# Issue order and spreading of the side work in the sequence stage of a gated Fourier and GEGLU kernel

## The chip, the cores and the metric

The kernel runs on one core of one Trainium2 chip. The metric is the device time of one execution in microseconds; the time before is the median of three runs. All arithmetic is float32, done on TensorE (PE) as three products of split numbers: each operand is a high part and a low part, and a product of two split operands is three matmuls (high by high, low by high, high by low). VectorE is DVE, ScalarE is ACT, GpSimd is POOL, SyncE is SP; SP does nothing here but issue DMAs.

## The reference

```python
x = A_x                                   # 1 x 2048 x 640
g = sigmoid((x * gate_w).sum(-1, keepdims=True))
a = einsum("bsd,ed->bse", x, dft_hid_re)
b = einsum("bsd,ed->bse", x, dft_hid_im)
A = einsum("ts,bse->bte", dft_seq_re, a) - einsum("ts,bse->bte", dft_seq_im, b)
B = (gelu(x @ w_gate) * (x @ w_up)) @ w_down        # F = 1728
return g * A + (1 - g) * B
```

## The kernel before

The kernel computes products in 2 by 2 blocks by a Strassen scheme with seven products, so each stage needs sums and differences of its operands ahead of its matmuls. It has four stages, one after the other on PE:

- **Gate and up** (line 1238): 13 blocks of F. The last one, `f = 12`, also prepares the next stage: its DVE and ACT side jobs wait in the list `fills`, and `fill` (line 1214) lets them out in step with PE, by their written costs (`state["all"]`, `state["pe_all"]`): a job is let out when the cost done so far is at most 1.25 x all x pe / pe_all. Within this stage the order on PE, ACT, DVE and POOL is the written one.
- **C stage** (line 1368): the sequence DFT applied to x, with the products kept in HBM (`uA`, and their sums `uT`). It has 64 steps: four groups of 16 (cosine or sine, and two halves of t). In a group the first eight steps (`b = 0`, "first half") have 30 matmuls each and use the x factors `xa`; the last eight (`b = 1`, "second half") have 24 and use `xb`. A step `i` needs its two tiles of DFT matrix c(i), 512 KB each.
- **K stage** (line 1505): the down projection, from h (`hA`, `hT`) and `w_down` (`wd`, and its sums `wsd`).
- **U stage** (line 1563): the hidden DFT, from `uA`, `uT`, `wu` and its sums `wsu`, and the mix of both branches.

**A C step.** In step `i` the program writes `load_c(i + 3)` (line 772: two loads on SP), then `split_c(i + 2)` (line 779: in a first-half step two high parts on ACT, line 80, and two low parts on DVE, line 83; in a second-half step also four differences on DVE into `csa` and `csb`, lines 785 to 789), then the 10 or 8 products of step `i`. In the first eight steps it also loads and splits the x factors: `fetch_xn` loads (line 739), `split_xa` makes three differences on DVE, a high part on ACT, and the low part by a negation on ACT and an accumulating DMA on POOL (`by_dma`, line 754); `whole=True` would make the low part on DVE.

**The transition in a group.** The last first-half step (`held`, line 1394) is written otherwise: PE does X, ACT copies X out of PSUM, then comes `prepare` (the split of c(i+2), whose high parts are on ACT), then the other products, then ACT copies Z and L out. The first second-half step needs PSUM banks that these copies free (`pQ`). ACT and DVE run in written order in this stage, so the copy of Z stands behind the high parts of c(i+2), and these stand behind what DVE has ahead of their differences. PE, POOL and SP have no written order here: the framework's scheduler places their instructions by its own estimate, with each instruction allowed ahead of an earlier one when its tile is free.

**Units.** The C stage also does side work for the later stages. A unit's loads are written in one step and its DVE work in the next step (`ready`, line 1373), behind `prepare`, with stores on POOL:

- T sums of h (`sum_h`, line 615): four loads of 256 KB, four DVE sums, four stores. Steps by `HT_AT`, four units for each of the last three groups.
- weight sums (`sum_wd`, line 608): loads `dr` (512 KB) and `da`, four DVE sums, four stores to `wsd`. Steps by `WD_AT`, two for each of these groups.
- logits (`load_z`, line 719): a load `xz` of 320 KB and one DVE reduction. Steps by `ZC_AT`.
- `sum_wu` (line 679): loads `ur` and `ua`, sums, stores to `wsu`; in steps `WU_AT` and the next.

Behind each second half DVE forms the group's results and, in the next step, `tsums` (line 1486), which POOL stores to `uA` and `uT`.

**Tiles.** Loads wait for free tiles: tag `s4` has 46 (c, x factors, `dr`, `xz`), tag `m` has 15 (`ht`, `ur`, the group's results), tag `w` has 6 (`da`, `ua`).

`in_order(SP)` (line 106) adds an edge from each SP instruction traced inside it to the next one, so that the scheduler must keep the written order; nothing is added on the chip.

Of the kernel before, what the change touches and what calls it, by code (L numbers as in the profile page):

```python
# [21 lines left out]
NP = NS // 2  # L22
NF = F // P
# [4 lines left out]
PAIRED = 3  # L28
ZB_AT = [5,7,9,14,15,16]
XB_AT = [0, 1, 2, 3, 4, 5, 6, 7]  # L30
WU_AT, WU_DOWN = [18, 34, 50], [10, 17]
HL_AT = [1, 12]


# [1 line left out]
def kernel(  # L36
# [636 lines left out]
    def store_left():  # L673
        for to, v in left_out:
            nc.sync.dma_start(to, v)
        left_out.clear()
# [62 lines left out]
    def fetch_xn(sp):  # L739

        r, s = xraw[sp] = tuple(slot(F32, [P, 4, 256], f"x{k}{sp}") for k in "nm")
        nc.sync.dma_start(r[:, 0:3], xn[sp, :, 0:3])
        nc.sync.dma_start(s[:, 0:2], xn[sp, :, 3:5])
# [259 lines left out]
    loads = ExitStack()  # L1003
# [208 lines left out]
    fills, state = deque(), {}  # L1212
# [24 lines left out]
    with in_order(PE, ACT, DVE, POOL):  # L1237
        for f in range(1, NF):
            kind = pair_of(f)
            if f == PAIRED:  # L1240
                loadu()
                fills.extend([*t4, *u123[:3], *late_work, *u123[3:], *u4])
            fills.extend(todo)
            todo.clear()
            if kind == 1:
                up, work = make_up(f, load_up(f))
                fills.extend(work)
            if f == PAIRED - 1:
                loadp()
                fills.extend(t123)  # L1250
            if f + 1 < NF:
                nxt, work = make_w(f + 1)
                if kind != 1 or f == PAIRED:
                    fills.extend(work)
            if kind == 1 and f > PAIRED:
                fills.extend(work)
            if f == NF - 1:
                for k in range(2):
                    fetch_xn(k)
                    load_c(k)  # L1260

                def made():
                    sums_made.pop(0)()

                for k in range(2):
                    fills.extend([(126, partial(split_xa, k)), (122, made), (245, partial(split_c, k))])
            state.update(pe=0, done=0, all=sum(c for c, _ in fills), pe_all=2450 if not kind else 2994 if kind == 1 else 1768)
            s5 = pair(F32, f"s5{f}")
            xs = {}
            work = [gate_up(f, W, Bs[tp], tp, s5[:, tp], s1t, xs, s4) for tp in range(2)]  # L1270
            more = together(f, W, Tp, s1t, xs) if kind == 1 else iter(())
            more_up = together_up(f, W, up, s4) if kind == 1 else iter(())
            store_left()
            if f == 2:
                k = len(fills) // 2
                rest = [fills.pop() for _ in range(len(fills) - k)]
                fills.extend([*sum_h0(0), *sum_h0(1), *reversed(rest)])
                state["all"] = sum(c for c, _ in fills)
            for _ in range(4):
                run(more)  # L1280
            for step in range(8 if not kind else 7):
                for tp, w in enumerate(work):
                    run(w)
                    if (step, tp) in ((0, 1), (1, 1)):
                        run(more)
                        if step == 0:
                            run(more)
                    if (2, 0) < (step, tp) < (6, 0):
                        run(more_up)
                if step < 2 and kind == 1 and f > PAIRED:  # L1290
                    for k in ((1,), (2, 3))[step]:
                        load_across(f, "xu", Tu, keptu, k)
                if step == 4 and pair_of(f + 1) == 1 and f + 1 > PAIRED:
                    for k in (1, 2, 3):
                        load_across(f + 1, "xq", Tp, keptp, k)
                if step == 5:
                    load_w(f + 2)
                if f == NF - 1 and step == 5:
                    fetch_xn(2)
                    load_c(2)  # L1300
            for v in (more, more_up):
                next(v, None)
            while fills:
                fills.popleft()[1]()
            W = nxt
# [49 lines left out]
    def put(to, i, src):  # L1355
        nc.gpsimd.dma_start(to[:, i], src)

    HT_AT, WD_AT, ZC_AT = {}, {}, [17, 22, 30, 33, 38, 46, 49, 53, 54, 62]
    for g in range(3):
        for q, r in enumerate((2, 3, 4, 13)):  # L1360
            HT_AT[16 * g + 16 + r] = q % 2, 2 * g + q // 2
        for q in range(2):
            WD_AT[16 * g + 18 + 2 * q] = 2 * g + q
    units = []
    X = Z = V = L = Q = R = Y = None
    sv, wus = {}, {}
    store_left()
    for i, (j, ri, b, sp) in enumerate(cseq):
        if i + 3 < NP:
            fetch_xn(i + 3)  # L1370
        if i + AHEAD + 1 < len(cseq):
            load_c(i + AHEAD + 1)
        ready, units = units, []
# [4 lines left out]
        if i in ZC_AT:  # L1378
            (_, first), (_, total) = load_z(1)
            first()  # L1380
            units.append(total)
        if i + 2 < NP:
            split_xa(i + 2, False)
        for _ in range(XB_AT.count(i)):
            split_xb(xleft.pop(0))

# [56 lines left out]
        else:  # L1443
# [21 lines left out]
            if lst:  # L1465
# [32 lines left out]
                        put(to, 3, t4)  # L1498

                after.append(tsums)  # L1500


    zwork, narrow = [], []
    gates(0)
# [266 lines left out]
```

## Time and profile before

| | us |
|---|---|
| median of three runs (lowest, highest) | 1059.74 (1057.55, 1061.1) |
| profiled execution, its own time | 1058.28 |
| span of that execution, first to last instruction | 1056.5 |
| PE busy in the span | 1024.0 |
| DVE, ACT, POOL busy | 823.8, 487.9, 185.0 |
| C stage on PE, first c matmul to first K matmul | 331.02 to 762.08 |
| mean granted TensorE clock | 0.989 |

A row of the waits view reads: who waited, for whom, total us, times, longest us. A row of the windows view reads: stretch in us from the span's start, its length, then busy us of PE, PEld, DVE, ACT and POOL with their number of instructions, the granted clock, the DMA share and GB/s. A row of the timeline reads: start, duration, engine, line, operation, out<-in, count, and in brackets the idle time before it with what ended it; an SP row is the issue of a DMA. A row of the groups reads: line, engine, operation, out<-in and shapes, count, then busy us and mean ns, then idle us before. A row of the issues view ends with the size of one transfer and the median us from issue to landing.

### The profile page before, as it was taken

To read this page: it belongs to the slowest core of one execution; us is meant where nothing else is said; L and a number is where in the kernel's file an instruction comes from. 1 tells how busy PE (TensorE), PEld (TensorE's weight loads), DVE (VectorE), ACT (ScalarE), POOL (GpSimd) and SP (SyncE) were. 2 spreads that over 40 slices of the span, in tenths; PEclk is the share of its full clock that TensorE was granted. 3 is DMA by queue.
4 is the path that set the end of the run, shared out by engine and by line. 5 is a ranking of instruction groups with operands and counts; after the bars stand their busy time and mean duration, and the time that the engine had idled before them with its cause. 6 is when DMAs were issued, how large, how long until landed. Compare 5 with 4: busy or idle time off the path is not lost.

```text
span 1056.5 us, 13360 instructions
## 1 busy us (share of the span) xinstructions
PE 1024.0 (97%) x4489; PEld 839.9 (79%) x4489; DVE 823.8 (78%) x1158; ACT 487.9 (46%) x625; POOL 185.0 (18%) x327
## 2 busy tenths in 40 slices
PE   9999999999999999996999799998999999999998
PEld 7888888888888778885888678876888878888887
DVE  8977755474759689767887798789989797996796
ACT  6644535444436654423343244324537636654340
POOL 0221111111301110223023301240120111011112
PEclk9999999999999999999999989998999999999999
DMA  8465455454669956898789877999899999987856
GB/s 308 146 213 193 126 179 166 152 167 147 195 208 331 252 163 231 263 385 308 258 283 384 340 265 256 382 413 361 294 327 372 412 391 341 391 316 218 269 151 100
DMA packets 101332, 281.47 MB, mean 266 GB/s; under 512 B 13520, under 2 KB 24656, under 8 KB 101264
## 3 DMA queue, kind: packets, MB, share of 16 engines
q1 hardware_dynamic: 73536, 194.15, 52.4%
q0 software_dynamic: 27440, 86.28, 25.7%
q8 instruction: 35, 0.57, 0.2%
q14 instruction: 33, 0.27, 0.1%
q10 hardware_dynamic: 288, 0.20, 0.1%
HBM read 205.06 MB, written 70.27 MB: 261 GB/s over the span
## 4 chain that ended last, share of the span: by engine, by line
PE 62%; issue 16%; DMA 16%; DVE 3%; POOL 2%; ACT 0%; SPq 0%; POOLq 0%; DVEq 0%
DMA ht<-hA 4%; PE pX L99 4%; PE pX L101 4%; PE pX L100 4%; DMA xz<-in_xz 4%; PE pZ L101 3%; PE pZ L100 3%; PE pZ L99 3%; DMA cra<-in_ct 2%; DMA crb<-in_ct 1%; DMA uA<-s 1%; PE kX L99 1%; PE kX L101 1%; PE kX L100 1%; PE kL L100 1%
## 5 line engine op out<-in xcount | busy, mean ns | idle before, releaser
L80 ACT ACTIVATE ch<-csa 128x1024 fp32r<-128x1024 f32 x32 | 34.0, 1062 | 123.8 <-DVE csa L786 102.0
L80 ACT ACTIVATE ch<-cra 128x1024 fp32r<-128x1024 f32 x32 | 33.9, 1059 | 78.8 <-DMA cra<-in_ct 32.9
L83 DVE TENSOR_TENSOR cl<-cra,ch 128x1024 fp32r<-128x1024 f32 x32 | 39.1, 1221 | 24.1 <-ACT ch L80 15.8
L415 POOL DMA_DIRECT2D hA<-s x48 | 26.1, 545 | 177.6 <-DVE s L582 158.0
L415 POOL DMA_DIRECT2D hT<-ht x48 | 26.0, 541 | 144.4 <-DVE ht L623 134.6
L99 PE MATMUL pL<-ch,xah 128*128 128x512 f32 x128 | 50.0, 391 | 0.5 <-DVE sa L1469 0.5
L100 PE MATMUL pL<-cl,xah 128*128 128x512 f32 x128 | 49.8, 389 | 0.0
L101 PE MATMUL pL<-ch,xal 128*128 128x512 f32 x128 | 49.0, 389 | 0.0
L571 DVE TENSOR_TENSOR s<-s,pX 128x512 f32<-128x512 f32 x24 | 16.4, 685 | 38.5 <-PE pX L101 38.5
L83 DVE TENSOR_TENSOR cl<-crb,ch 128x1024 fp32r<-128x1024 f32 x32 | 39.1, 1222 | 9.1 <-ACT ch L80 3.8
L80 ACT ACTIVATE ch<-crb 128x1024 fp32r<-128x1024 f32 x32 | 33.8, 1057 | 25.0 <-PE pL L100 10.3
L83 DVE TENSOR_TENSOR cl<-csa,ch 128x1024 fp32r<-128x1024 f32 x32 | 39.0, 1220 | 2.9 <-ACT ch L80 2.5
L99 PE MATMUL pQ<-ch,xbh 128*128 128x512 f32 x64 | 26.7, 417 | 13.9 <-ACT s L146 13.9
L83 DVE TENSOR_TENSOR cl<-csb,ch 128x1024 fp32r<-128x1024 f32 x32 | 39.2, 1224 | 0.7 <-PE pY L100 0.2
L557 ACT ACTIVATE s<-pZ 128x512 f32<-128x512 f32 x24 | 14.2, 597 | 52.2 <-PE pZ L101 35.3
L576 ACT ACTIVATE s<-s 128x512 f32<-128x512 f32 x24 | 15.1, 633 | 46.8 <-DVE s L575 46.8
L80 ACT ACTIVATE ch<-csb 128x1024 fp32r<-128x1024 f32 x32 | 33.9, 1060 | 6.2 <-DVE csb L789 5.2
L99 PE MATMUL pX<-ch,xbh 128*128 128x512 f32 x64 | 25.6, 406 | 9.7 <-ACT ch L80 6.3
L146 ACT ACTIVATE s<-pX 128x512 f32<-128x512 f32 x41 | 23.7, 593 | 24.5 <-PE pX L101 24.2
L83 DVE TENSOR_TENSOR kl<-kw,kh 128x1024 fp32r<-128x1024 f32 x24 | 29.3, 1223 | 5.4 <-ACT kh L80 5.4
L80 ACT ACTIVATE kh<-kw 128x1024 fp32r<-128x1024 f32 x24 | 25.5, 1063 | 16.2 <-DMA kw<-wsd 13.8
L99 PEld LDWEIGHTS pL<-ch,xah 128*128 128x128 f32 x128 | 24.0, 188 | 6.3 <-DVE sa L1469 1.3
(3658 smaller groups left out, 3475.1 us busy)
## 6 DMA issues: line engine op xcount, KB each, us to landing
cra<-in_ct SPq DMA_DIRECT2D x64, 512.0 KB, 5.9
crb<-in_ct SPq DMA_DIRECT2D x64, 512.0 KB, 7.0
hA<-s POOLq DMA_DIRECT2D x48, 256.0 KB, 3.0
ht<-hA SPq DMA_DIRECT2D x48, 256.0 KB, 8.3
hT<-ht POOLq DMA_DIRECT2D x48, 256.0 KB, 6.9
kr<-hA SPq DMA_DIRECT2D x24, 512.0 KB, 7.4
kr<-hT SPq DMA_DIRECT2D x24, 512.0 KB, 8.3
ux<-uA SPq DMA_DIRECT2D x24, 512.0 KB, 7.3
```

Source lines behind the costliest of these rows:

```text
L80: nc.scalar.activation(hi, raw, AF.Copy)
L83: nc.vector.tensor_tensor(lo, raw, hi.bitcast(F32), op=ALU.subtract)
L99: nc.tensor.matmul(ps, lh, rh, start=first, stop=False, skip_group_check=True)
L100: nc.tensor.matmul(ps, lh, rl, start=False, stop=False, skip_group_check=True)
L101: nc.tensor.matmul(ps, ll, rh, start=False, stop=last, skip_group_check=True)
L146: nc.scalar.activation(m, src, AF.Copy)
L415: nc.gpsimd.dma_start(to[:, i], src)
L557: nc.scalar.activation(s5, Z, AF.Copy)
L571: tt(s5, s5, X, op=ALU.add)
L576: nc.scalar.activation(s2, s2, AF.Gelu_apprx_tanh)
```

## The change

Five edits, all for the C stage:

1. SP keeps the written order from the first to the last step of the C stage.
2. T sums: the places in a group move from steps 2, 3, 4 and 13 to 2, 4, 8 and 13. Weight sums: from 2 and 4 to 3 and 5.
3. Logits: from steps 17, 22, 30, 33, 38, 46, 49, 53, 54, 62 to 16, 22, 26, 32, 38, 42, 48, 54, 58, 60 (in places of a group: 1, 6, 14 / 1, 6, 14 / 1, 5, 6, 14 become 0, 6, 10 / 0, 6, 10 / 0, 6, 10, 12). The third `sum_wu` moves from step 50 to 49.
4. The third x factor `xa[2]` is made in the last block of gate and up, with its low part on DVE; two entries (126 and 122) join the six of `fills`. Its loads go out at step 3 of that block and those of x factor 3 at step 5.
5. In the C stage the x factors are loaded four steps ahead and split three steps ahead, each one step earlier than before.

```diff
-WU_AT, WU_DOWN = [18, 34, 50], [10, 17]
+WU_AT, WU_DOWN = [18, 34, 49], [10, 17]
...
                 for k in range(2):
                     fills.extend([(126, partial(split_xa, k)), (122, made), (245, partial(split_c, k))])
+                fills.extend([(126, partial(split_xa, 2)), (122, made)])
...
+                if f == NF - 1 and step == 3:
+                    fetch_xn(2)
                 if f == NF - 1 and step == 5:
-                    fetch_xn(2)
                     load_c(2)
+                    fetch_xn(3)
...
-    HT_AT, WD_AT, ZC_AT = {}, {}, [17, 22, 30, 33, 38, 46, 49, 53, 54, 62]
+    HT_AT, WD_AT, ZC_AT = {}, {}, [16, 22, 26, 32, 38, 42, 48, 54, 58, 60]
     for g in range(3):
-        for q, r in enumerate((2, 3, 4, 13)):
+        for q, r in enumerate((2, 4, 8, 13)):
             HT_AT[16 * g + 16 + r] = q % 2, 2 * g + q // 2
         for q in range(2):
-            WD_AT[16 * g + 18 + 2 * q] = 2 * g + q
+            WD_AT[16 * g + 19 + 2 * q] = 2 * g + q
...
     store_left()
+    loads = ExitStack()
+    loads.enter_context(in_order(SP))
     for i, (j, ri, b, sp) in enumerate(cseq):
-        if i + 3 < NP:
-            fetch_xn(i + 3)
+        if i + 4 < NP:
+            fetch_xn(i + 4)
...
-        if i + 2 < NP:
-            split_xa(i + 2, False)
+        if i + 3 < NP:
+            split_xa(i + 3, False)
...
                 after.append(tsums)
-
+    loads.close()
```

## The prediction, made before the change was run

> **What bounds the kernel now.** I read the page first, then the waits of PE, then a table by half groups of the C stage, and last the queues around one stall.
>
> ```profile
> PE 1024.0 (97%) x4489; PEld 839.9 (79%) x4489; DVE 823.8 (78%) x1158; ACT 487.9 (46%) x625; POOL 185.0 (18%) x327
> ```
>
> PE is the bound, so only time in which PE idles or runs slowly can be gained. Its waits, longest in total first:
>
> ```profile
> PE pQ L99 <- ACT s L146: 13.9, 2, 7.4
> PE pX L99 <- ACT ch L80: 6.3, 2, 6.0
> PE pX L99 <- ACT s L146: 3.4, 3, 1.5
> PE pX L101 <- DMA xal<-xn: 2.3, 2, 1.6
> ```
>
> All are in the C stage, on tiles that first appear where a first half turns into a second half, or on an x factor's low part. The windows by half groups (first and second half of each group; the third row is a stretch without stalls):
>
> ```profile
> 331.02:389.84 58.82, 56.54 (x247) 45.93 (x246) 44.40 (x65) 35.77 (x38) 7.45 (x10) 1.00 0.81 228
> 389.84:434.71 44.87, 44.10 (x193) 35.88 (x192) 39.76 (x47) 22.97 (x27) 2.22 (x4) 1.00 0.67 226
> 402.07:434.71 32.64, 32.64 (x145) 27.03 (x144) 27.65 (x32) 15.78 (x18) 0.00 (x0) 1.00 0.62 207
> 434.71:490.63 55.92, 54.57 (x241) 44.86 (x240) 42.85 (x62) 15.59 (x17) 20.01 (x37) 1.00 1.00 351
> 490.63:544.31 53.68, 45.99 (x193) 37.35 (x193) 43.44 (x55) 22.95 (x27) 4.87 (x9) 0.94 0.78 261
> 544.31:600.95 56.64, 54.86 (x241) 44.78 (x240) 45.07 (x65) 15.78 (x17) 20.54 (x38) 1.00 1.00 371
> 600.95:653.60 52.65, 45.91 (x193) 37.30 (x194) 43.18 (x55) 22.50 (x27) 4.32 (x8) 0.90 0.72 251
> 653.60:709.25 55.65, 54.86 (x242) 44.78 (x240) 44.98 (x65) 17.42 (x22) 21.45 (x40) 1.00 1.02 384
> 709.25:762.08 52.83, 46.52 (x192) 37.74 (x193) 48.91 (x63) 24.66 (x29) 4.49 (x9) 0.94 0.92 339
> ```
>
> The third row gives 32.64 / 144 = 0.2267 us a matmul without a stall (six steps of 24). A first half of 240 matmuls then takes 54.40, a second half of 192 takes 43.52. So the halves lose, in order: 3.06 (six gate and up matmuls are in that stretch: 55.76), 1.35, 1.52, 10.16, 2.24, 9.13, 1.25 and 9.31; 38.0 in all, and 33.6 of it from the first half of group 1 on. That is the most the change can win.
>
> Where does a stall of about 10 come from? SP around the transition of group 1, which is at 490:
>
> ```profile
> 467.01 0.33 SPq L611 DMA_DIRECT2D dr<-in_wd  x1
> 477.45 0.33 SPq L612 DMA_DIRECT2D da<-in_wd  x1
> ...
> 481.09 0.46 SPq L777 DMA_DIRECT2D crb<-in_ct  x1
> 481.64 0.49 SPq L726 DMA_DIRECT2D xz<-in_xz  x1
> 495.44 0.33 SPq L612 DMA_DIRECT2D da<-in_wd  x1
> ```
>
> Nothing is issued from 467.01 to 477.45, and nothing from 481.64 to 495.44. Each time a load `da` ends the gap. By the count of these loads in the queue they are the fifth and the sixth of six, which belong to the weight sums written in steps 50 and 52; these are steps 22 and 24. The scheduler put them 28 steps ahead. The waits of SP name what it stood for:
>
> ```profile
> SPq L777 <- PE pY L101: 105.6, 25, 6.3
> ...
> SPq L612 <- DMA wsd<-da: 23.3, 2, 13.3
> ```
>
> A `da` waited for a tile of tag `w` until the store of an earlier one had landed, and the c tiles stood behind it: the loads of c(24), c(25) and the logit row went out together from 477.87 on. What followed, from the chain, DVE, ACT and PE:
>
> ```profile
> 481.64 13.59 DMA xz<-in_xz
> ```
>
> ```profile
> 495.26 0.83 DVE L730 CUSTOM_DVE_ANT_0 xz<-xz,gwb 128x640 f32<-128x640 f32 x1 [3.91 <-DMA xz<-in_xz]
> ```
>
> ```profile
> 499.62 1.07 ACT L146 ACTIVATE s<-pZ 128x512 f32<-128x512 f32 x2
> ```
>
> ```profile
> 500.25 0.80 PE L99 MATMUL pQ<-ch,xbh 128*128 128x512 f32 x1 [7.42 <-ACT s L146]
> ```
>
> The row lands 13.59 us after its issue, the logit's reduction is ahead of the differences of c(25) on DVE, their high parts are ahead of the copy of Z on ACT, and PE's `pQ` needs that copy: 5.0 us from the landing (495.23) to 500.25.
>
> **The change, part by part.**
>
> *SP in written order, with the units spread.* At the transition PE would reach `pQ` without a stall at 490.5: 490.63, less the 1.5 that the first half lost, plus six matmuls. Less 5.0, c(25) and the logit row must have landed by 485.5. Both are written in step 22. The second half begins at 490.63, 1.5 of it a wait, and steps 22 and 23 are 30 matmuls each: step 22 starts at 490.63 - 1.5 - 2 x 6.80 = 475.5. Loads of c wait for tiles that PE frees at the end of a step (25 waits for `pY`), so they go out at the step's start; the logit row, third in the queue, by about 476.8. That leaves 8.7 us to land. The nearest rows for the latency:
>
> ```profile
> cra<-in_ct SPq DMA_DIRECT2D x64, 512.0 KB, 5.9
> ...
> ht<-hA SPq DMA_DIRECT2D x48, 256.0 KB, 8.3
> ```
>
> Between 5.9 and the 13.59 above I take 10, nearest to the loads of the T sums, which run in the same halves, because one T sum unit (eight transfers of 256 KB, 2.1 MB) leaves the first half: 384 GB/s x 55.65 = 21.4 MB becomes 19.3 MB in 54.4, 355 GB/s. So each of three transitions keeps 1.3, say 1.5, of its stall; the bounds are 0 (5.9) and 5 (13.59).
>
> The other moves have one answer: weight sums a step later, the third `sum_wu` a step earlier, logits up to four earlier change no count on DVE, POOL or SP, and a first half leaves DVE 9 to 11 us (54.40 less 42.85 to 45.07) to take them at another step. Without that room a logit would cost its 0.83. Behind them on SP stand the next c loads, half a microsecond an issue.
>
> The clock is a term too. The stall of 7.42 stands in a half that lost 10.16, so about 2.7 went with matmuls at the lower clock (0.94 in that half, against 1.00 in the first row, whose gap was 1.6). Held in proportion, 0.37 for each us of gap, three gaps of 1.5 would add 1.7. The first row's gap of 1.6 left the clock at 1.00, so I add nothing and keep 1.7 for the range. The Trainium skill ("TensorE: Matmul & The Clock Gate", What's actually happening) says that the clock halves only after an idle window of about 3.4 us; by that the sum below stays 1033.3, by the proportion it would be 1035.0.
>
> *DVE in the second halves.* A half without units has DVE busy for 39.76 (second window row), so 43.52 leave 3.8. Price of a unit:
>
> ```profile
> L83 DVE TENSOR_TENSOR cl<-csb,ch 128x1024 fp32r<-128x1024 f32 x32 | 39.2, 1224 | 0.7 <-PE pY L100 0.2
> ...
> L629 DVE TENSOR_TENSOR ht<-ht,ht 128x512 f32<-128x512 f32 x12 | 8.3, 692 | 0.4
> ```
>
> A T sum is 4 x 0.69 = 2.8. After the change each of the last three second halves holds two (5.5) and a logit (0.83): 46.1 against 43.5, a debt of 2.6 that is paid out of the lead of DVE over PE and recovered in the next first half (42.85 to 45.07 busy, less 2.8, in 54.40). Over a whole group DVE is busy 86.3, 88.3 and 93.9 of 97.9, so it can just keep up if it seldom waits. I charge 1.0 a group; bounds 0 and 2.6.
>
> *Entry into K.* DVE's results of the last group must empty banks:
>
> ```profile
> 760.87 1.37 DVE L1469 TENSOR_TENSOR sa<-s,pQ 128x512 f32<-128x512 f32 x2 [1.10 <-ACT s L146]
> ```
>
> ```profile
> 765.03 0.39 PE L99 MATMUL kV<-kb0001h,kh 128*128 128x512 f32 x1
> ```
>
> DVE was early by 1.10 there because the stall at 709 had let it catch up. That half held 48.91 of DVE work and gains 2.8, and 43.52 are 8.2 too short for it; the split of one second-half c tile, 4 x 0.69 + 2 x 1.22 = 5.2, is done ahead of the half when its loads are in time. So these sums start about 3 + 1 later, and `kV`, 2.95 behind the first K matmul, waits for some of that: +2, bounds 0 and 4.
>
> *The third x factor.* The waits for `xal` (2.3, with their tails most of the 3.06) go: its low part no longer comes by the accumulating DMA, and the later factors are made one step, 6.8, earlier. -2.9, bounds -1.0 and -3.0. Of the 1.35 behind it, part came from the order that the wait forced: -0.4, bounds 0 and -1.35. But the two new entries raise the list's cost from 986 to 1234, so the older ones are let out sooner: threshold 1.25 x 1234 / 1768 = 0.87 of PE's ns instead of 0.70. Worked through with PE's 136, 204, 136 and 68, the high part of `xa[1]` moves from pe = 952 to 816, ahead of the first copy of X, and c(1) from 1088 to 952, ahead of the second. ACT, before:
>
> ```profile
> 322.90 0.60 ACT L146 ACTIVATE s<-pX 128x512 f32<-128x512 f32 x1 [0.24 <-PE pX L101]
> 325.21 1.06 ACT L80 ACTIVATE xah<-xn 128x1024 fp32r<-128x1024 f32 x1 [1.72 <-DVE xn L752]
> 326.18 0.58 ACT L146 ACTIVATE s<-pX 128x512 f32<-128x512 f32 x1
> ```
>
> ```profile
> 326.81 0.49 PE L99 MATMUL pX<-xT13h,ws12h 128*128 128x512 f32 x1
> ```
>
> The high part waits for DVE until 325.21 anyway, so the first copy slips to 326.2 (it ended at 323.5), then two high parts of c(1), about 1.0 each, then the second copy to 328.6 to 329.2. PE's product at 326.81 needs that second copy: +2.4, bounds 0 (if the scheduler has other matmuls to put there) and 4 (if DVE's extra 3 x 0.4 + 1.2 delays the last results as well).
>
> **The sum**, against the profiled execution's 1058.28: three transitions and the small stalls at the starts of groups, -33.6 + 3 x 1.5 + 3 x 1.0 = -26.1; K +2; x factors -2.9 and -0.4; gate and up +2.4. Together -25.0, 1033.3. The median of the runs is 1.5 above that execution, so I say 1034. The terms' bounds, all at one end, give 1021 and 1054.
>
> **The rivals.**
>
> *The loads stay late.* SP's blocks go, but the c tiles still can't be issued before tiles are free, and land after 12 to 14 us because the first halves still move 355 GB/s. For it: 105.6 us of SP's waits are for tiles that PE frees; the DMA share is 1.00 to 1.02 in these halves; and group 3 lost its 9.31 although all `da` loads were behind it by then. Against it: after 481.64 SP waited 13.8 us for `da`, not for a tile of c, and the third T sum's 2.1 MB, 5.5 us at 384 GB/s, leave group 3 too. Each transition then loses about 5 and DVE, without its wait, pays 2 more: 1058.3 - 33.6 + 15 + 6 + 2 - 3.3 + 2.4 = 1047. The Trainium skill ("Perfetto Trace Analysis", Optimization Strategy) says that a gap which repeats can mean too little memory for the next tile; that is this rival's reading, and no order on SP would cure it.
>
> *Head-of-line blocking at step 18* (the slower side). In written order `ht` and `ur`, six tiles of tag `m`, stand ahead of every later c load. Twelve of the fifteen hold the last group's results until the stores to `uT` land. If that is past the start of step 19 by as much as the `da` wait (13.8), c(22) to c(25) are late by it, and the old block of 10.4 comes back longer in each group: 3 x 3.4 + 2.4 - 3.3 = +9.3, 1067. Against it, both `ur` loads went out at the end of step 17 and early in step 18:
>
> ```profile
> 447.26 3.40 SPq L685 DMA_DIRECT2D ur<-in_wu  x2
> ```
>
>  It decides from a wait of about 5 us past the start of step 19 on; below that, leads hide it.
>
> *No change in effect.* If the loads that matter stand in written order already, the edges do nothing, and x factors and gate and up cancel: 1058.3 - 3.3 + 2.4, about 1058. Against it, a `da` stands 28 steps ahead of its place, which an ordered queue can't hold.
>
> **How the numbers follow.** Forecast 0.66, loads stay late 0.20, blocking 0.09, no effect 0.05. The range reaches from 1024 (the forecast with three of its terms at their good ends) to 1051 (the second case with its spread); what it leaves out is the last two cases and the ends of the first, under 2 in 10. The forecast's own range is 1024 to 1043. About 0.3%, 3 us, is what a measurement of this kernel can tell from no change: faster 0.86, same 0.05, slower 0.09.
>
> **What would show it.** Right: the C stage's second halves at 44 to 46 us with the clock at 1.00; the SP queue without gaps of 10 us, `da` only behind its own `dr`; `pQ` waiting under 3; no wait for `xal`; one new wait of PE for a copy of X near 326. Wrong: `pQ` still waiting for 5 or more behind a logit row or c tile (second case), or SP standing for `ht` or `ur` for over 10 (third). If second halves keep PE waiting for `cl` at every step, I have DVE's debt too small; if K opens with a gap, its size is that term.

## The result, and the profile after

| | before | after |
|---|---|---|
| median, us (lowest to highest) | 1060.42 (1057.55 to 1061.82, 4 runs) | 1053.36 (1051.62 to 1054.85, 4 runs) |
| profiled execution, its span | 1058.28, 1056.5 | 1054.85, 1053.1 |

The ratio is 0.9936, with a 95% interval of 0.991 to 0.9963: faster by 0.6%, 7 us and not 25, and outside the range of 1024 to 1051.

The page and the waits of PE after:

```profile
PE 1024.7 (97%) x4489; PEld 841.8 (80%) x4489; DVE 824.7 (78%) x1159; ACT 486.3 (46%) x624; POOL 184.8 (18%) x326
```

```profile
PE pX L99 <- ACT ch L80: 11.8, 3, 8.5
PE pQ L99 <- ACT s L146: 5.6, 1, 5.6
PE kZ L99 <- DVE ksa L985: 4.4, 1, 4.4
```

The waits for `xal` are gone. At the transitions PE still waits for 17.4; `pQ` waits less, and `pX` for a c tile's high part (`ch`) more. One wait is new in its size, `kZ` in the K stage. The windows by half groups (first half, second half, and so on; the first begins earlier than before and ends at the first matmul of group 0's second half):

```profile
325.27:386.85 61.58, 61.49 (x271) 50.60 (x270) 50.52 (x69) 38.70 (x44) 6.60 (x9) 1.00 0.84 249
386.85:432.17 45.32, 44.09 (x193) 35.88 (x192) 39.47 (x47) 23.51 (x27) 2.23 (x4) 1.00 0.66 222
432.17:487.29 55.12, 54.56 (x241) 44.86 (x239) 38.37 (x54) 15.59 (x17) 16.29 (x30) 1.00 0.92 335
487.29:542.58 55.29, 46.52 (x193) 37.69 (x193) 48.35 (x65) 21.79 (x25) 8.70 (x16) 0.91 0.79 268
542.58:597.00 54.42, 54.42 (x242) 45.05 (x240) 42.25 (x60) 16.82 (x19) 18.46 (x34) 1.00 1.00 374
597.00:645.22 48.22, 45.46 (x194) 37.07 (x192) 45.82 (x60) 21.36 (x24) 6.52 (x12) 0.96 0.85 293
645.22:699.64 54.42, 54.42 (x242) 45.04 (x240) 41.98 (x59) 18.69 (x24) 18.24 (x34) 1.00 1.01 376
699.64:751.24 51.60, 45.98 (x194) 37.58 (x193) 48.85 (x65) 24.43 (x28) 7.82 (x15) 0.93 0.96 369
```

Against 54.40 and 43.52 the second halves lose 1.8, 11.8, 4.7 and 7.9 (before 1.4, 10.2, 9.1 and 9.3); group 1 lost more than before. (The last row runs to the end of the last c matmul, 0.16 past K's first one at 751.08; that 0.16 is not counted here.) The later first halves lose 0.7, 0.0 and 0.0 (1.5, 2.2, 1.3), and the opening one nothing: its 271 matmuls (31 of gate and up among them) take 271 x 0.227 = 61.5.

Why group 1? SP's queue is as it was meant to be:

```profile
467.45 0.41 SPq L611 DMA_DIRECT2D dr<-in_wd  x1
467.91 0.44 SPq L612 DMA_DIRECT2D da<-in_wd  x1
472.94 0.33 SPq L777 DMA_DIRECT2D cra<-in_ct  x1
473.36 0.38 SPq L777 DMA_DIRECT2D crb<-in_ct  x1
480.38 0.33 SPq L726 DMA_DIRECT2D xz<-in_xz  x1
```

Each `da` stands behind its `dr`. The logit row goes out 7.0 us behind c(25), with which it is written: SP stood 6.6 of them for an s4 tile that a low part on DVE had to leave (the one at 479.13 below). The time from issue to landing of the two loads that mattered, one load in each row, the second of c(25) (issued at 473.36) and the logit row (480.38):

```profile
DMA to landing us min/median/max: 7.8/7.8/7.8
```

```profile
DMA to landing us min/median/max: 2.8/2.8/2.8
```

So c(25) was there at 481.1 and the row at 483.2, ahead of the 485.5 that I had asked for; before it was 495. Yet PE stood still. DVE, then ACT, POOL and PE, in the trace after:

```profile
479.13 1.23 DVE L83 TENSOR_TENSOR cl<-crb,ch 128x1024 fp32r<-128x1024 f32 x1 [7.94 <-DMA wsd<-dr]
...
490.39 0.69 DVE L785 TENSOR_TENSOR csa<-cra 128x512 f32<-128x512 f32 x1
```

```profile
496.88 1.06 ACT L80 ACTIVATE ch<-csb 128x1024 fp32r<-128x1024 f32 x1 [4.04 <-DMA wsd<-dr]
497.84 1.07 ACT L146 ACTIVATE s<-pZ 128x512 f32<-128x512 f32 x2
```

```profile
473.01 1.14 POOL L604 DMA_DIRECT2D wsd<-dr  x2 [1.25 <-DMA hT<-ht]
...
489.95 1.14 POOL L604 DMA_DIRECT2D wsd<-dr  x2
```

```profile
489.11 0.39 PE L101 MATMUL pX<-ch,xbl 128*128 128x512 f32 x1
497.98 1.22 PE L99 MATMUL pX<-ch,xbh 128*128 128x512 f32 x2 [8.49 <-ACT ch L80]
499.00 0.63 PE L99 MATMUL pQ<-ch,xbh 128*128 128x512 f32 x1
499.43 0.63 PE L100 MATMUL pQ<-cl,xbh 128*128 128x512 f32 x1
```

A low part of c(23) was to be written into an s4 tile in which an earlier unit still lay: `dr`, whose results POOL was storing to `wsd`. Until those stores had landed, DVE stood for 7.94, and all that was written behind it stood too: a T sum, the split of c(24), a weight sum, the logit, and only at 490.39 the differences of c(25). (In the last first-half step a unit's work stands ahead of `prepare`, not behind it.) Then the last high part of c(25) waited 4.04 for the next weight sum's stores, and the copy of Z behind it went at 497.84. The scheduler had put two X products that need this part ahead of `pQ`; either way PE's release is that high part. In the trace before neither DVE nor ACT has a wait for `wsd<-dr` in the C stage.

Groups 2 and 3 are another case. DVE has no such wait there; it waits for the logit row, and PE's product follows it by the old chain. Group 2, then group 3, DVE and PE in the trace after:

```profile
596.71 0.83 DVE L730 CUSTOM_DVE_ANT_0 xz<-xz,gwb 128x640 f32<-128x640 f32 x1 [1.56 <-DMA xz<-in_xz]
```

```profile
601.28 0.79 PE L99 MATMUL pX<-ch,xbh 128*128 128x512 f32 x2 [2.76 <-ACT ch L80]
```

```profile
701.79 0.83 DVE L730 CUSTOM_DVE_ANT_0 xz<-xz,gwb 128x640 f32<-128x640 f32 x1 [2.10 <-DMA xz<-in_xz]
```

```profile
706.78 0.79 PE L99 MATMUL pQ<-ch,xbh 128*128 128x512 f32 x1 [5.62 <-ACT s L146]
```

From the row to PE it is 4.6 and 5.0 us, as in the prediction. But six matmuls into the second half, less 5.0, is 593.4 and 696.0, and the rows landed at 596.7 and 701.8, 3.3 and 5.8 too late. In group 2 the row went out at 589.35, behind a c load for which SP had stood 6.5 until stores `wsd<-dr` landed; in group 3 it went out at 690.16 and took 11.6.

And the K stage. Its first matmul and the first one into the banks that its first half frees, before and after:

```profile
762.08 0.39 PE L99 MATMUL kX<-kb0000h,kh 128*128 128x512 f32 x1
```

```profile
847.99 0.50 PE L99 MATMUL kZ<-kb1001h,kh 128*128 128x512 f32 x1 [0.73 <-DVE ksa L985]
```

```profile
751.08 0.39 PE L99 MATMUL kX<-kb0000h,kh 128*128 128x512 f32 x1
```

```profile
842.18 0.80 PE L99 MATMUL kZ<-kb1001h,kh 128*128 128x512 f32 x1 [4.40 <-DVE ksa L985]
```

K begins 11.0 earlier, that product 5.8 earlier, and the span ends 3.4 earlier. So two thirds of what the C stage gained was lost again behind it. (These two executions stand 3.4 apart, the medians 7.1; the tallies below are of the executions.)

### The profile page after: what moved, and what is told of

It is laid out like the page before. It is cut to its first block, busy times and chain, and to the rows that moved or that the text cites. A ratio compares the mean times of both kernels' runs of the same rounds, so it can differ in the third digit from the quotient of the medians.

```text
span 1053.1 us, 13358 instructions
## 1 busy us (share of the span) xinstructions
PE 1024.7 (97%) x4489; PEld 841.8 (80%) x4489; DVE 824.7 (78%) x1159; ACT 486.3 (46%) x624; POOL 184.8 (18%) x326
## 4 chain that ended last, share of the span: by engine, by line
issue 27%; PE 25%; DMA 7%; POOL 5%; DVE 2%; ACT 1%; SPq 0%; POOLq 0%; DVEq 0%; ACTq 0%
DMA xz<-in_xz 2%; POOL hT L415 1%; POOL uA L1359 1%; POOL uT L1359 1%; DMA ua<-in_wu 1%; DMA crb<-in_ct 1%; DMA ht<-hA 1%; DMA wneg<-ur 1%; PE yX L101 1%; PE yX L99 1%; PE yX L100 1%; PE kX L99 1%; DMA wsd<-dr 1%; PE kX L101 1%; PE kX L100 1%
## 5 line engine op out<-in xcount | busy, mean ns | idle before, releaser
L415 POOL DMA_DIRECT2D hT<-ht x48 | 26.1, 544 | 157.5 <-DVE ht L623 149.4
L99 PE MATMUL pX<-ch,xbh 128*128 128x512 f32 x64 | 25.4, 405 | 12.3 <-ACT ch L80 11.8
L80 ACT ACTIVATE kh<-kw 128x1024 fp32r<-128x1024 f32 x24 | 25.5, 1064 | 21.8 <-DMA kw<-wsd 21.8
L101 PEld LDWEIGHTS pL<-ch,xal 128*128 128x128 f32 x128 | 24.0, 188 | 5.0
```

The lines of the kernel that those rows point to most:

```text
L80: nc.scalar.activation(hi, raw, AF.Copy)
L99: nc.tensor.matmul(ps, lh, rh, start=first, stop=False, skip_group_check=True)
L101: nc.tensor.matmul(ps, ll, rh, start=False, stop=last, skip_group_check=True)
```

## The experiments

Theory of the held tile: order and spreading did free SP, but put c tiles' parts into tiles that stores to `wsd` hold, and DVE and ACT, in written order, pass that wait on to the copy of Z. Its rivals: the loads are late whatever is done; the written order at the transition makes large stalls of small delays; and K gives back what C gains.

Losses below are of the second halves of groups 0 to 3 (stretch less 192 matmuls) and, in brackets, of the first halves of groups 1 to 3 together, in us, from the traces, good to 0.2. The last second half is taken to the end of the last c matmul, which adds 0.16 to each kernel where K follows at once. A wait of the first product of a second half counts to the first half ahead of it.

| kernel | median | ratio to before (95%) | second halves (first halves) |
|---|---|---|---|
| before | 1060.4 | | 1.4, 10.2, 9.1, 9.5 (5.0) |
| after | 1053.4 | 0.9936 (0.991 to 0.9963) | 1.8, 11.8, 4.7, 8.1 (0.8) |
| x factors alone | 1059.0 | 0.9974 (0.9955 to 0.9994) | 1.8, 9.8, 8.4, 9.6 (5.6) |
| order on SP alone | 1065.5 | 1.0033 (1.0006 to 1.006) | 1.4, 10.7, 8.3, 8.7 (10.7) |
| after without the order | 1064.4 | 1.0032 (1.0011 to 1.0053) | 1.8, 10.2, 7.8, 4.1 (11.6) |
| dr in tag m | 1044.5 | 0.984 (0.9795 to 0.9886) | 1.8, 4.1, 3.7, 5.9 (0) |
| results of dr in tag m | 1044.2 | 0.9828 (0.9792 to 0.9865) | 1.8, 2.5, 4.7, 8.1 (0) |
| fourth sum_wu late | 1047.8 | 0.9874 (0.9823 to 0.9925) | 1.8, 12.4, 4.6, 8.2 (0.8) |
| dr in tag m, sum_wu late | 1038.4 | 0.9785 (0.976 to 0.9809) | 1.8, 2.8, 4.1, 6.1 (0) |
| split behind the copies, on after | 1042.4 | 0.9827 (0.9806 to 0.9848) | 0, 1.1, 4.2, 2.4 (4.1) |
| all three | 1033.8 | 0.9737 (0.971 to 0.9764) | 0, 0.8, 0.9, 1.6 (2.9) |

**The tile of `dr`.**

```diff
-        r, a21 = slot(F32, [P, 8, P], f"dr{k}"), wsmall(F32, f"da{k}")
-        nc.sync.dma_start(r, wd[k, :, :8])
+        r = [mtile(F32, f"dr{k}{q}").rearrange("p (b c) -> p b c", c=P) for q in range(2)]
+        a21 = wsmall(F32, f"da{k}")
+        for q in range(2):
+            nc.sync.dma_start(r[q], wd[k, :, 4 * q : 4 * q + 4])
```

> The kernel after, with the weight sum's 512 KB operand dr in two tiles of tag m (256 KB each) instead of one of tag s4. Theory of the held tile: in group 1 of the kernel after, DVE's low part of c(23) waited 7.94 us and ACT's high part of c(25) 4.04 us for the stores wsd<-dr, whose tile they had been given; without dr in s4 both waits go, the 8.49 us gap of PE at 497.98 shrinks under 2, the C stage gets 8 to 11 us shorter, and the time is 1042 to 1046 if the K stage keeps what it gets. Rival, late loads: the c tiles and logit rows land too late whatever holds the tiles, so the gap at the transition of group 1 stays 6 or more and the time is 1052 to 1055. Rival, the K stage takes it back: the C stage is 8 to 11 shorter, but PE's wait for ksa in the K stage (4.40 in the kernel after) grows by about as much, and the time is 1050 to 1053.

Measured 1044.5: the held tile, and K takes back no more than it did. The gap of 8.49 is one of 2.21 here, a little over the 2 of the theory. No DVE or ACT instruction of the C stage waits for `wsd<-dr` here. PE's waits:

```profile
PE pQ L99 <- ACT s L146: 8.1, 3, 4.1
PE kZ L99 <- DVE ksa L987: 4.3, 1, 4.3
```

The wait for `ksa` stays what it was although K starts another 11 earlier, so it is no fixed date set by the loads. What is left at the transitions is the row: in group 1 it goes out at 475.1, takes 10.6, and lands 2.3 too late by the same reckoning.

A control, for dr's load is halved here and tag s4 has more room:

```diff
-        r, a21 = slot(F32, [P, 8, P], f"dr{k}"), wsmall(F32, f"da{k}")
+        r, a21 = pool.tile([P, 8, P], F32, tag="dr", name=f"dr{k}", bufs=2), wsmall(F32, f"da{k}")
...
-        return pool.tile(shape, dt, tag="s4", name=name, bufs=46)
+        return pool.tile(shape, dt, tag="s4", name=name, bufs=44)
```

> The kernel after with dr, still one load of 512 KB, in a tag of its own with two tiles, and two tiles fewer (44) for tag s4. Held tile: no c tile can be given dr's tile, so no DVE or ACT instruction of the C stage waits for wsd<-dr, and the time is near that of dr in tag m (1044.5): 1042 to 1048, two tiles fewer costing up to 3. If dr in tag m helped because its loads were halved or because tag s4 had more room: the time stays at 1051 to 1056, as in the kernel after.

Measured 1056.9 (0.9962, 0.9943 to 0.9981): just over the rival's numbers, though the waits for `wsd<-dr` are gone, and group 1's second half lost 7.7. The two tiles that s4 gave up cost it elsewhere: C starts 2.0 later than in the kernel after, and the second half of group 0 loses 6.2 in place of 1.8. SP waits longer for tiles that DVE's low parts have to leave:

```profile
SPq L777 <- DVE cl L83: 92.5, 34, 10.1
```

In the kernel after that is 22.5. The control mixed two effects, and a cleaner one was needed, which keeps dr's load and its tile in s4 and lets it go when DVE has used it:

```diff
+            o = own[0] = [mtile(F32, f"dw{k}{q}").rearrange("p (b c) -> p b c", c=P) for q in range(2)]
+            tt(o[0][:, 0:2], a21, a22, op=ALU.add)
+            tt(a21, a11, a21, op=ALU.subtract)
...
+            tt(o[0][:, 2:4], o[0][:, 0:2], a11, op=ALU.subtract)
+            tt(o[1][:, 0:2], a12, o[0][:, 2:4], op=ALU.subtract)
```

> The kernel after with dr still loaded into a tile of tag s4, but three of the four results of a weight sum written into two tiles of tag m, from which POOL stores them; so dr's tile is free when DVE has done the sums, not when the stores have landed (6.9 to 8 us later). Held tile: DVE and ACT no longer wait for wsd<-dr, group 1's transition loses 4 to 7 in place of 11.7, and the time is 1043 to 1049. Shortness of tiles: dr's tile is still taken from its load to its sums, the waits come back under other names, and the time is 1050 to 1055.

Measured 1044.2, and group 1 loses 2.5, less than the 4 to 7 expected. So it is the hold by the stores: 9 of the 18 us that the prediction missed in C. Groups 2 and 3 lose 4.7 and 8.1 as in the kernel after: there the rows take 12.1 and 9.9 to land and are 3.5 and 6.4 too late.

**Order and spreading, each alone.**

> The kernel before, with SP in written order in the C stage and nothing else of the change. The prediction gave this edit, with the spreading, 26 us. Held tile: the order takes the gaps of 10 us out of SP's queue and brings da back behind its own dr, but DVE and ACT then wait for wsd<-dr at the transitions instead, so the time falls by 0 to 5 only (1055 to 1060). If the order alone makes the whole gain: 1053 to 1055. If it costs (blocking at ht and ur in steps 18 and 19, with T sums still in steps 2, 3 and 4): above 1061.

> The kernel after without the written order on SP; T sums, weight sums, logits and x factors stay as in the kernel after. If the order makes the gain: da loads are hoisted again, SP's queue has gaps of 10 us again, and the time is 1057 to 1060 (the x factors' 2.5 stay). If the spreading makes it: 1051 to 1055, the order being worth nothing. Held tile: the stalls of groups 1 to 3 stay 5 to 12 us each either way, behind da in this kernel and behind wsd<-dr in the kernel after.

The first kernel is the one before with the two lines of `in_order(SP)` around the C stage, the second the one after without them. Both are slower than the kernel before, by 0.3%: the first as the expectation had it if the order costs (above 1061), the second outside its forecasts. With the order alone `da` is in its place, but the row of step 22 goes out at 478.06, behind four c loads from 471.65 on, and takes 14.5 us to land; DVE:

```profile
492.57 0.82 DVE L730 CUSTOM_DVE_ANT_0 xz<-xz,gwb 128x640 f32<-128x640 f32 x1 [2.53 <-DMA xz<-in_xz]
```

That is my rival of the late loads, in this kernel. No wait of SP at a load `ht` or `ur` is over 2.5 there, so it is not the blocking that the expectation named. Without the order a `da` goes out 7 us behind its `dr` again, and ACT waits for dr's stores 28.1 us in four waits; the longest:

```profile
481.79 1.06 ACT L80 ACTIVATE ch<-cra 128x1024 fp32r<-128x1024 f32 x1 [14.49 <-DMA wsd<-dr]
```

So in group 1 the row is in time only with both, and dr's tile is in the way with either: DVE and ACT wait for `wsd<-dr` 8.1 us with the order alone, 28.1 with the spreading alone, and not at all before. Not all of the second kernel's loss is in C: its K begins 2.1 earlier than before, and from there to the end it takes 7.1 longer.

**dr in tag m, on the kernel before**, and **the x factors alone** (edits 4 and 5 of the change):

> The kernel before with dr in two tiles of tag m, and nothing of the change. In the kernel before neither DVE nor ACT waited for wsd<-dr; SP's queue waited for da there. Held tile: the edit pays only where SP is in order, so here the stalls of about 10 stay and the time is 1056 to 1062. If dr's tile costs whatever the order of SP: 1048 to 1054.

> The kernel before with the x factor edits alone (the third factor in gate and up, its low part on DVE, the others loaded and split a step earlier). The prediction gave them 2.9 and 0.4 less 2.4 of gate and up, 0.9 together. In the kernel after PE stood 2.5 ahead of the kernel before at the end of the first group, and gate and up lost nothing: so 1057 to 1059 if the gain is carried to the end, and 1060 to 1062 if the stall of the next transition takes it back.

Measured 1061.7 (1.0003, 0.998 to 1.0026) and 1059.0. The tile costs nothing where `da` holds up SP, as expected; and the x factors are worth what the trace after shows, about 2, carried to the end.

**The loss in K.** Ahead of the sums that free the banks, DVE in the kernel after had this:

```profile
835.11 0.43 DVE L597 TENSOR_TENSOR ur<-ua,ur 128x256 f32<-128x256 f32 x1 [2.52 <-DMA wneg<-ur]
...
840.24 1.29 DVE L985 TENSOR_TENSOR ks<-ks,ks 128x512 f32<-128x512 f32 x2
```

```diff
-WU_AT, WU_DOWN = [18, 34, 49], [10, 17]
+WU_AT, WU_DOWN = [18, 34, 49], [12, 17]
```

> The kernel after with the fourth sum_wu two steps of the K stage later (step 12 instead of 10). In the kernel after, DVE waited 2.52 us at 835.11 for its stores wneg<-ur, did its four sums (1.7 us), and 4.4 us later PE got the banks that the sums of the first half of K free (kZ for ksa, 4.40 us at 842.18). If that wait and these sums are what made ksa late: kZ's wait falls to under 1.5 and the time to 1049 to 1051. If the K stage is held by its loads (DMA share 1.01 to 1.04 there), DVE only waits elsewhere instead: kZ's wait stays 3 or more, and the time is 1052 to 1055.

Measured 1047.8, better than both. The sums start earlier, and PE no longer waits for `ksa`; DVE in this kernel:

```profile
835.52 1.29 DVE L985 TENSOR_TENSOR ks<-ks,ks 128x512 f32<-128x512 f32 x2
```

I had counted the wait alone. The 12 matmuls behind it ran for 5.3 us in place of 2.7, so the wait cost 4.4 + 2.6 = 7.0, and the span fell by 1053.1 - 1046.0 = 7.1. ACT waits as long for `kw<-wsd` in both (21.8 and 21.9), so what the edit gave did not come from the loads.

Why DVE is late there at all is open. PE's earlier arrival alone is not the reason: with the spreading and without the order K begins 2.1 earlier than before, not 11.0, and still

```profile
PE kZ L99 <- DVE ksa L985: 3.6, 1, 3.6
```

Counted from K's first matmul, the first `ksa` comes after 85.2 us before, 90.4 after and 89.5 in that kernel. Up to `kZ` ACT waits for `kw<-wsd` 10.4, 18.4 and 18.5, so late loads of the weight sums may have a part in it; no run here separates that.

> The kernel after with both edits that helped alone: dr in two tiles of tag m, and the fourth sum_wu in step 12 of the K stage instead of 10. Medians so far: after 1053.4, the first edit alone 1044.5 (8.9 less), the second alone 1047.8 (5.6 less). If the two losses are independent (held tile in C, DVE's wait ahead of the bank-freeing sums in K): 1038 to 1041, PE's wait for ksa gone and the transitions as in the first edit. If the K stage is held by its loads and takes back what C gains: kZ waits again for 3 or more and the time is 1042 to 1045.

Measured 1038.4: the two losses are independent (8.9 and 5.6 make 14.5; 15.0 measured).

**The order at the transition.** What is left is in the row of `pQ` above: the logit row lands late, and the copy of Z stands behind all that waits for it. With dr in tag m, the last high part of c(25) and the copy of Z on ACT:

```profile
489.26 1.06 ACT L80 ACTIVATE ch<-csb 128x1024 fp32r<-128x1024 f32 x1 [0.23 <-DVE csb L791]
490.23 1.07 ACT L146 ACTIVATE s<-pZ 128x512 f32<-128x512 f32 x2
```

```diff
                     sv["c11", d] = copy(X[d], f"s1{n}{d}")
-                prepare()
...
                 put(uA[j][4], 2 * ri + 1, l2)
+                prepare()
```

> The kernel of the pair of edits (dr in tag m, the fourth sum_wu late) with the split of c(i+2) in the last first-half step written behind the copies of Z and L and the sum with V, instead of ahead of them. With dr in tag m PE still waited 8.1 us in three waits (longest 4.1) for pQ behind the copy of Z, which stood behind the high part of c(25), which stood behind the logit row's reduction on DVE. If that order is what is left of the transitions: the waits for the copy of Z fall under 1 each, and the time is 5 to 9 under the pair. If the tile of c(i+2) is then late for its own step: a wait for ch or cl of 2 to 4 us one step later in each group, and the time is within 3 of the pair.

> The kernel after with the split of c(i+2) in the last first-half step behind the copies, and nothing else. Held tile alone: the parts of c(23) and c(25) still wait 7.9 and 4.0 us for wsd<-dr, c(25) is ready at about 498.5, and the wait of step 24 (11.7 lost) only moves to step 25: 1049 to 1053. Order as the amplifier: PE enters step 24 when c(24) is ready (about 488) and has 5.4 us of it to do before it needs c(25), so group 1 loses 5 to 6, group 2 under 2 (4.7 in the kernel after) and group 3 under 4 (7.9), 12 to 14 less in C; with the K stage's 4.4 still there: 1039 to 1044.

> The kernel before with that same move of the split behind the copies, and nothing of the change. In the kernel before c(25) and the logit row landed at 495 at the transition of group 1, c(25) was ready about 499, and step 25 could begin at 496 at the earliest. Order as the amplifier: each transition loses 3 to 4 in place of 9 to 10, and the time is 1041 to 1046. If the late tile itself is the limit: the waits move to step 25 with their size, and the time is 1055 to 1060.

All three edits together: 1033.8, 4.7 under the pair, just short of the 5 to 9 forecast. The rows land as late as in the pair (11.2, 12.1 and 10.5 us after their issue, 11.0, 9.7 and 10.5 in the pair), but PE no longer waits for them. The longest waits of PE in its C and K stages:

```profile
PE kZ L99 <- DVE sa L1476: 4.4, 1, 4.4
PE pL L99 <- DVE sa L1476: 2.0, 2, 1.1
PE pX L99 <- ACT s L146: 1.3, 2, 0.7
```

The transitions are all but gone (0 to 1.6), and part of it comes back where DVE's results empty banks: 1.5 and 1.4 at the starts of groups 2 and 3, and 4.4 at the entry of K. On the kernel after the move alone gives 11.0 (1042.4), the time that the order as amplifier forecast, but not its picture: the groups lose 1.1, 4.2 and 2.4, where 5 to 6, under 2 and under 4 were forecast. With the move the parts of c were also given other tiles: the waits of DVE and ACT for `wsd<-dr` fall from 11.9 to 0.7, and DVE stands for 7.65 in group 2 instead. So the 11.0 is not the order's alone; the 4.7 on the pair, which hardly has such waits, is. On the kernel before the move gave 1056.9 (0.9964, 0.9943 to 0.9986), the number of the late tile, and again not its picture: its second halves lose 8.6, 5.8 and 4.6, about 10 less in all, and of the 10.6 by which K begins earlier 5.5 are lost behind that. So the change is worth 14.5 us once this order is out of the way, and 7 with it.

> The kernel after with the split of c(i+2) in the last first-half step behind the copies, and the fourth sum_wu in step 12 of K; dr stays in tag s4. Sum of the single effects (1053.4 less 11.0 less 5.6): 1036 to 1038, and then dr's tile is worth 2 to 4 beside them (1033.8 with all three). If the later K entry leaves the fourth sum_wu nothing to give: 1040 to 1042.

Measured 1037.9 (0.9764, 0.9734 to 0.9793), the sum of the single effects. DVE here still waits for dr's stores, in group 2:

```profile
577.63 1.23 DVE L83 TENSOR_TENSOR cl<-crb,ch 128x1024 fp32r<-128x1024 f32 x1 [7.45 <-DMA wsd<-dr]
```

The second half that follows loses 4.7, and 0.9 with dr in tag m: without the copies behind it, such a wait costs PE 4, where dr's tile cost 9 in group 1 of the kernel after (11.8 against 2.5). The two are not quite alike, for there a second wait of 4.04 followed the first. Four is also the difference of the two medians.

> The kernel before with SP in written order and the split behind the copies; nothing spread, x factors as before. The kernel before with the split behind the copies took 1056.9, the kernel after with it 1042.4. If the order on SP makes that difference: 1042 to 1048 (the x factors' 2.5 are missing). If the spreading makes it: 1054 to 1060.

> The kernel after without the order on SP and with the split behind the copies; units spread, x factors as in the kernel after. If the spreading makes the difference of 14.5: 1042 to 1046. If the order on SP makes it: 1052 to 1058. If each alone is worth nothing, as without the move of the split: both this and the run with the order alone at 1054 to 1060.

Measured 1056.5 (0.9951, 0.9928 to 0.9975) and 1063.8 (1.0025, 1.0 to 1.005): neither part makes the 14.5, they need each other with this move as without it. The second number is above all that was expected for it. Of the 14 that the first kernel loses in its later first halves, 12.5 stand at the transitions: the first product of the second half waits 4.49, 1.80 and 6.21 for the copy of X. In group 1 that copy stands on ACT behind the high parts of c(24), whose second load kept DVE waiting for 1.95: late loads again, one step earlier.

**A last one**, for the entry of K: the fourth T sum of the last group in step 54 instead of 61, on top of all three.

```diff
-        for q, r in enumerate((2, 4, 8, 13)):
+        for q, r in enumerate((2, 4, 8, 13 if g < 2 else 6)):
```

> The kernel of the pair of edits with the split behind the copies (1033.8), with the last group's fourth T sum in step 54 instead of 61. There PE waited 4.4 us at the entry of K for sa, the last group's result on DVE. If DVE's work in the last second half makes that wait, 2.8 us of it (four sums of 0.69) leave: kZ's wait falls to 1 to 2 and the time by 2 to 3, to 1030.5 to 1032. If the first half, whose DMA share is about 1, pays for it: a new wait for ch or cl in steps 54 to 57 and the same time, 1033 to 1035.

Measured 1032.5 (0.9739, 0.9716 to 0.9761) beside 1033.8 (0.9737): no difference that these runs resolve. The wait at K's entry fell to 1.6, as the first theory had it, but a new one stands at step 56, as the second had it, for a result instead of a c tile:

```profile
691.72 0.50 PE L99 MATMUL pR<-ch,xbh 128*128 128x512 f32 x1 [1.96 <-DVE s L1444]
```

## Why the prediction was wrong

**The transitions, -33.6 + 4.5 + 3.0.** This is the step that failed. The blocks of SP and their cause were read rightly, and the order put `da` back. What failed is "Less 5.0, c(25) and the logit row must have landed by 485.5", with 1.5 left for each of three transitions, and it failed in two ways. In group 1 c(25) and the row landed in time, but the 5.0 from landing to PE did not hold. I had taken it out of one stall, in which DVE and ACT had nothing else late; it is a chain of written-order work, and it is that short only if DVE is ready for it. In the kernel after it was 497.98 - 483.2 = 14.8, since DVE had been held up for 7.94 and ACT waited 4.04 more. In groups 2 and 3 the chain held (4.6 and 5.0), but the rows landed 3.3 and 5.8 too late, where my 10 us of latency and "by 476.8" had allowed for 1.3. From the start of its step I had given the row 1.3 to go out; it took about 7, 6 and 4, in groups 1 and 2 because SP waited for tiles (6.6 and 6.5).

The clock, at which "I add nothing", was a term too: the matmuls right behind the gaps of 8.49, 2.76 and 5.62 lost 2.4, 1.7 and 2.1 by their slower pitch.

The three transitions with the first halves kept 25.1 (0.7 + 11.8 + 4.7 + 7.9) of the 33.6; I had left them 7.5. The runs with dr's results elsewhere, and with the split behind the copies, show both halves of it: the tile makes the delay in group 1, the late row makes it in groups 2 and 3, and the order makes it PE's: with dr in tag m and `sum_wu` late, the move takes the losses from 2.8, 4.1 and 6.1 to 0.8, 0.9 and 1.6.

**"The other moves have one answer."** They had not. I had counted instructions of the moved weight sums on DVE, POOL and SP, but not how long their tile is held: from the load to the landing of the last store, with DVE's and ACT's next tiles as possible heirs.

**DVE's debt, 1.0 a group**, did not show in the kernel after (its group starts lose 0.0): the stalls that stayed let DVE catch up. Where they are gone it is there, 1.5 and 1.4.

**K.** The entry cost 0.2 rather than 2, for the same reason; without stalls it is 4.4, over my bound of 4. The wait for `ksa`, 91 us further on, was missing in the sum: 3.7 more than before and the slow matmuls. In the trace before it stood with 0.73, the mark of a DVE that is just in time; in the kernel after, counted from K's start, DVE comes there 5.2 later. The fourth `sum_wu` ahead of it is a part that a run shows; what else made DVE later is open. I had looked for what DVE owes at the entry of K and no further.

**The x factors, -2.9 and -0.4, gate and up +2.4.** The waits for `xal` went, 3.06 with their tails; the 1.35 became 1.8. Gate and up lost nothing, my bound "if the scheduler has other matmuls to put there": C's first matmul is at 325.27, among them. Together -2.6 in place of -0.9.

**The sum**, then: transitions -8.5, the first group -2.5, and +7.6 from K's entry to the end, -3.4 between the two executions, where I had -26.1, -0.9 and +2. (The forecast itself was a little off in its last step: 1033.3 and 1.5 make 1034.8, not 1034.)

**The rivals.** Late loads (1047) was the nearest in its number, and half right in its mechanism: in the kernel after the loads of group 1 were in time, but the rows of groups 2 and 3 were late, and the 4.7 and 7.9 lost there are what it meant by "about 5". Its sign, `pQ` waiting for 5 or more behind a logit row, is there in group 3 (5.62). The evidence stood in the prediction: group 3 had lost 9.31 with all `da` loads behind it. In the kernel with the order alone it was so in group 1 too. What it cites from the Trainium skill ("Perfetto Trace Analysis", Optimization Strategy), that a repeating gap can mean too little memory for the next tile, bears on this in two places: SP's loads waited for tiles, as I had put it (6.6 and 6.5), and so did the parts that DVE and ACT write (7.94 and 4.04). In the second place it was not the number of tiles but how long stores held one. Blocking at `ht` and `ur` did not come in the kernel after.

The number of all three edits, 1033.8, is the one that I forecast for the change alone; that is chance, since it holds the gains of the fourth `sum_wu`, of dr's tile and of the moved split, which I had not seen.

## What to carry to other kernels

When a queue is freed, follow the tile and not only the transfer: who holds the tile that the next result needs, until which store has landed, and what stands behind that wait in a written order. A deadline that is worked out at one transition has to be checked at each of them. A copy that frees the next products' banks should not be written behind work that nobody needs yet; here that move took 4.7 off the pair of edits and 11.0, with other tiles, off the kernel after. And when side work is moved, look through the rest of the program for waits that are nearly zero: each is a place where another engine is just in time.

## What the runs showed of the hardware that I had not expected

A stall costs more than its length. In the traces of before and after and of the kernels that beat them, each gap of PE over 3.6 us in the C and K stages was followed by 6 to 14 matmuls at a pitch of 0.43 in place of 0.227 (the one at 497.98 above shows it): 1.3 to 2.9 us on top of the gap. Gaps of up to 1.65 with no other close behind left the pitch alone there, and between 1.8 and 2.9 it went either way: with dr in tag m seven slow matmuls came behind a gap of 1.82 (at 592.5), and after the split was moved on the kernel after none came behind one of 2.90. With dr in tag m, and with the pair of edits, the same product:

```profile
490.86 0.52 PE L99 MATMUL pQ<-ch,xbh 128*128 128x512 f32 x1 [2.21 <-ACT s L146]
...
492.03 0.63 PE L99 MATMUL pQ<-ch,xbh 128*128 128x512 f32 x1
492.45 0.63 PE L100 MATMUL pQ<-cl,xbh 128*128 128x512 f32 x1
```

```profile
491.10 0.50 PE L99 MATMUL pQ<-ch,xbh 128*128 128x512 f32 x1 [2.55 <-ACT s L146]
...
491.90 0.40 PE L99 MATMUL pQ<-ch,xbh 128*128 128x512 f32 x1
492.13 0.39 PE L100 MATMUL pQ<-cl,xbh 128*128 128x512 f32 x1
```

The shorter gap was followed by the slow pitch, the longer one not. The Trainium skill ("TensorE: Matmul & The Clock Gate", What's actually happening) has the clock halved after an idle window of about 3.4 us that runs freely; the gaps over 3.6 agree with it, and the slow matmuls behind 1.82 and 2.21 do not.

The same load of the logit row took 13.6 us before and 2.8 after, and 14.5 with the order alone. In the kernel after nothing had been issued on SP for 7 us ahead of it, in the other two four loads of c went out in the 7 us before; that this makes the difference is likely, but no run tests it alone.
